# Weight decoding in a Fourier and two-expert kernel: sign taken by a mask and added on GpSimd, two of its buffers closed by time, x queued ahead of weights, start-up and planner prices reordered

## The chip, the cores and the metric

One core of a Trainium2 chip. The metric is the device time of one execution in microseconds (us). The engines are TensorE (PE; its weight loads are PEld), VectorE (DVE), ScalarE (ACT), GpSimd (POOL) and SyncE (SP), which here only issues DMAs. Each works through its own list of instructions in order.

## The reference

```
X = fft(x, axis=1); X = fft(X, axis=2); x = X.real       # x is 2 x 3008 x 256
x = ((1/(1+exp(-(x @ w_gate)))) * (x @ w_val)) @ w_out    # width 1536
h = x @ w_in;  out = (h * cos(h)) @ w_out2                # width 2048, 6016 tokens
```

x is fp32. The host passes the weights as float64, so that the kernel itself turns each into fp32.

## The kernel before

**Stages.** The transform is three rounds of matmuls. Stage A reads x in 16 chunks of 8 matmuls (a pair of chunks is one x load into one of three buffers, `raw`); each fp32 matmul of this stage leaves two records in the trace, 256 in all, and four more come from `xs`. A chunk fills two of PSUM's eight banks, so chunks 3, 7, 11 and 15 use banks 6 and 7. Stage B (12 groups of 8 short matmuls, L405 and L406) and stage C (6 groups of 12, L443) follow, in the order that the string on L473 gives; C writes the transformed tokens into six buffers `eo`. The first expert then runs in 72 steps (`step1`): six token tiles by 12 slices of the hidden width. A step multiplies the two halves (`ab`, L499 to L501, two times six matmuls), DVE combines them (`even`, L517, two instructions; `tokens`, L525, two), ACT takes the sigmoid (L673), GpSimd multiplies (`times`, L529), ACT splits the product (L613, L614), and a GpSimd DMA with addition makes its low part (`lo1`, L552). Four steps later the PE multiplies it by the output weights (`out1`, L539 to L542). The second expert (192 slices, from about 490 us on) is not touched.

**Decoding.** A weight unit is 128 x 512 numbers, 512 KB as float64. SP loads it; ACT takes the magnitude of the high words (L129) and scales the low words (L130); DVE clamps (L113), shifts (L117) and puts the sign in (L135); GpSimd adds the rounding from the low words as integers (L138). A w1 unit then needs a sum and a difference (L159, L160). ACT copies the high part (L143) and DVE or GpSimd subtracts it for the low part (L144). L113 and L117 have one operand in SBUF and one constant in PSUM, which lies at the end of bank 7 (`cmax`, `cmask`); L135 has both operands in SBUF. A chunk that writes bank 7 waits for the last clamp or shift that was recorded ahead of it.

**Order.** Nothing is scheduled at run time. The kernel keeps a clock for each engine (`clk`), and at each stage's slot `fill` puts decode instructions into an engine's list as long as their planned end lies within the slot plus an allowance (`AHA`, `AHB`, `AHC`). A unit is decoded in a buffer that is free for a while: the `eo` buffers until stage C writes them (`ENDS`), and, once stage B has read half of `D1`, four pieces of it (`stages`). Two of those (`ALWAYS`) stay free; the other two are marked `TWO`, since step 2 writes its tokens over them, and whatever is still being decoded there is finished, instruction by instruction, ahead of `tokens` of step 2 on every engine that it needs.

Of the kernel before, what the change touches and what calls it, by code (L numbers as in the profile page):

```python
# [49 lines left out]
def fft_moe_moe(ctx: ExitStack, tc: tile.TileContext, x, x0, head, w1, w1s, wo1, w2, t1, t3, out):  # L50
# [69 lines left out]
    def dec_steps(buf, n):  # L120

        r = buf[:, 0:2 * n].rearrange("p (n t) -> p n t", t=2)
        lo, hi = r[:, :, 0], r[:, :, 1]
        t = buf[:, 2 * n:3 * n]
        u = t.bitcast(U32)

        return [

            (A, .52, lambda: A.activation(out=t, in_=hi, func=AF.Abs, scale=2.0 ** -80)),  # L129
            (A, .52, lambda: A.activation(out=lo.bitcast(I32), in_=lo.bitcast(U32), func=AF.Copy,  # L130
                                          scale=2.0 ** -29)),

            (V, .6, lambda: clamp(t)),
            (V, .6, lambda: shift(u)),
            (V, .6, lambda: V.scalar_tensor_tensor(out=u, in0=hi.bitcast(U32), scalar=0x80000000, in1=u,  # L135
                                                   op0=ALU.bitwise_and, op1=ALU.bitwise_or)),

            (G, 1.23, lambda: G.tensor_tensor(out=t.bitcast(I32), in0=t.bitcast(I32), in1=lo.bitcast(I32),  # L138
                                              op=ALU.add)),
        ]  # L140

    def hilo_steps(hi, lo, src):
        return [(A, .52, lambda: A.copy(hi, src)),  # L143
                (VG, .6, lambda e: e.tensor_tensor(out=lo, in0=src, in1=f32(hi), op=ALU.subtract))]  # L144

# [59 lines left out]
    def fill(e, until):  # L205

        while True:
# [8 lines left out]
            else:  # L216
                if e is DQ and len(todo) > held[0] and clk[e] + 1.5 <= until:
                    for bf in free:
                        if bf[2] <= until and max(clk[e], bf[2]) + LIFE <= bf[1]:
                            start(bf)  # L220
                            break
                    else:
                        return
                    continue
# [24 lines left out]
    LIFE, ALWAYS = 16.0, 1e9  # L249
    TWO = 1e8  # L250
    VADV = 0.5
    ENDS = (44, 52, 54, 62, 70, 70)

    AHA, AHB, AHC = (2, 1.5, 2, 2), (4, 1.5, 3, 1), (3, 1.5, 3, 0)

# [32 lines left out]
    with tc.tile_pool(name="xp", bufs=1) as xp:  # L288
# [23 lines left out]
        DQ.dma_start(out=raws[0][0:96, JC:2 * JC], in_=x[:, 1])  # L312
        G.memset(warm, 0.0)
        V.memset(hd[96:128], 0.0)
        V.memset(cmax, FMAX)
        V.memset(cmask, 0x7FFFFFFF)
        V.memset(hd2, 0.0)
        V.memset(raws[0][96:128], 0.0)
        G.memset(raws[1], 0.0)
        V.memset(raws[2], 0.0)  # L320
        V.memset(xs[96:128], 0.0)
# [4 lines left out]
        for p in range(1, NX2):  # L326
            fill(DQ, clk[DQ] + 2.0)
            load_x2(p)


        for _ in range(NWARM):
            PE.matmul(ps[:, 7, 0:128], warm, warm, start=True, stop=True)

        now = 3.5
        clk[V] = clk[G] = clk[A] = 4.5
        for c in range(NJC):
            if c == 8:
                DQ.dma_start(out=T1, in_=t1)
                DQ.dma_start(out=T3, in_=t3)
                spend(DQ, 1.4)  # L340
            slot(now, 1.71, AHA if c < NJC - 2 else (4, .4, 2, .5) if c < NJC - 1 else (4, .1, 2, -.8))
            b0 = 2 * (c % 4)
# [10 lines left out]
            if c % 2 and c // 2 + NX2 < NJC // 2:  # L353
                clk[DQ] = max(clk[DQ], now + 1.71)
                load_x2(c // 2 + NX2)

            def evac(c=c, b0=b0, at=now + (1.71 if c else 3.4)):
                src = ps[:, b0:b0 + 2, 0:384].rearrange("p a (q c) -> p c a q", c=96)
# [24 lines left out]
            after.append(evac)  # L383
            now += 1.71 if c else 3.4
    now += 1.2
# [13 lines left out]
    def stage_b(b, grp):  # L399
        slot(now, 1.71, AHB)  # L400
        bk = bank()
# [5 lines left out]

        def evac(at=now + 1.71):
            v = ps[:, bk, :].rearrange("p (q s k) -> p s q k", q=4, s=2)
# [21 lines left out]
        after.append(evac)  # L431
        return now + 1.71

    def stage_c(b, ch, ahead=AHB):
        slot(now, 2.54, ahead)
        t = b * NCH + ch
# [3 lines left out]
        def mm(terms, dst):  # L440
# [3 lines left out]

            def evac(at=now + 2.54):
                for un in list(live):
                    if un[1] and un[1][0] is flat[t]:
                        finish(un)
                if clk[V] + .59 < clk[A] + .2:
                    regular(V, .59, at)  # L450
                    V.tensor_copy(dst, o)
                else:
                    regular(A, .47, at)
                    A.copy(dst, o)
# [9 lines left out]
           eo[t][:, 1, 0:PC])  # L464
        return now + 2.54

# [6 lines left out]
    for st in "b00 b01 b02 b03 b04 c00 b05 b10 c01 b11 c02 b12 b13 b14 c10 b15".split():  # L473
# [354 lines left out]
```

## Time and profile before

| | |
|---|---|
| Median of 3 runs | 1028.24 us (1026.69 to 1030.5) |
| Profiled execution | 1028.23 us; its span 1026.3 us |
| Mean granted PE clock | 0.989 of full speed |
| Busy | PE 97%, DVE 75%, ACT 75%, POOL 65% |
| DMA | 85.59 MB, 83 GB/s on average |

Times in the profile count from the span's start; 1.9 us lie outside it. A busy PE is not a PE at its peak, but where its matmuls follow one another without a wait at full clock, the stretch can only be shortened by leaving matmuls out. What other work can move the time lies where PE waits or runs at half clock.

### The profile page before, as it was taken

The page shows a single profiled execution, that of the slowest core. Times are in us where ns is not written, and L with a number is a line of the kernel's source. Part 1 is how long each engine was busy: PE and PEld are TensorE (multiplying, and loading weights), DVE is VectorE, ACT ScalarE, POOL GpSimd, SP SyncE. Part 2 cuts the span into 40 slices and gives each one's busy share as a digit, 9 for nine tenths or more (in the row PEclk, how much of TensorE's full clock was granted, in tenths as well). Part 3 has the DMA queues.
Part 4 walks back from the last instruction along what each step waited for, and adds up shares of the span by engine and source line. Part 5 has one row for each costly group of instructions (what it writes and reads, how often), then busy time and mean ns, then how long its engine had stood idle before and what let it go on. Part 6 is the DMA issues. An engine that isn't in the chain of part 4 may idle for free.

```text
span 1026.3 us, 13186 instructions
## 1 busy us (share of the span) xinstructions
PE 996.3 (97%) x4566; PEld 831.8 (81%) x4566; DVE 770.0 (75%) x1031; ACT 765.4 (75%) x1207; POOL 667.7 (65%) x522
## 2 busy tenths in 40 slices
PE   7996899999999999999999999999999999999998
PEld 7984788887888888878788888888888888888886
DVE  5597887888878878786577777777777777777775
ACT  4675556756667676664788888888888888898886
POOL 3686687967878777775465665756557565665653
PEclk9998899999999999999999999999999999999999
DMA  9612456666676667778500000000000000000000
GB/s 293 226 62 82 81 129 134 141 155 150 146 158 139 136 160 155 187 196 219 130 1 21 1 21 21 1 20 1 21 21 1 21 1 21 0 21 21 1 21 22
DMA packets 25364, 85.59 MB, mean 83 GB/s; under 512 B 3248, under 2 KB 6640, under 8 KB 24624
## 3 DMA queue, kind: packets, MB, share of 16 engines
q0 software_dynamic: 10368, 37.02, 19.0%
q1 hardware_dynamic: 14672, 47.59, 13.6%
q8 instruction: 36, 0.59, 0.3%
q14 instruction: 32, 0.26, 0.1%
q10 hardware_dynamic: 256, 0.14, 0.0%
HBM read 33.16 MB, written 14.56 MB: 46 GB/s over the span
## 4 chain that ended last, share of the span: by engine, by line
PE 87%; DVE 4%; DMA 3%; ACT 2%; issue 2%; POOL 1%; ACTq 0%; SPq 0%; DVEq 0%; POOLq 0%
PE ps L581 25%; PE ps L499 14%; PE ps L500 14%; PE ps L501 14%; PE ps L539 5%; PE ps L541 5%; PE ps L542 5%; DVE D L525 3%; PE ps L349 2%; DMA gh<-D 1%; DMA raw<-in_x_dram 1%; PE ps L443 1%; ACT gh L613 1%; DMA xs<-in_x_dram 1%; PE ps L405 0%
## 5 line engine op out<-in xcount | busy, mean ns | idle before, releaser
L607 POOL TENSOR_TENSOR h<-D,h 128x502 fp32r<-128x502 f32 x191 | 284.2, 1488 | 215.9 <-ACT h L606 204.2
L581 PE MATMUL ps<-h,wr 128*128 128x502 f32 x1152 | 291.8, 389 | 0.0
L499 PE MATMUL ps<-es,wr 128*128 128x502 f32 x672 | 263.8, 393 | 17.3 <-DVE D L525 16.7
L500 PE MATMUL ps<-es,wr 128*128 128x502 f32 x672 | 262.8, 391 | 0.0
L501 PE MATMUL ps<-es,wr 128*128 128x502 f32 x672 | 261.9, 390 | 0.0
L581 PEld LDWEIGHTS ps<-h,wr 128*128 128x128 f32 x1152 | 217.4, 189 | 44.7
L529 POOL TENSOR_TENSOR D<-D 128x502 f32<-128x502 f32 x144 | 184.7, 1326 | 88.5 <-ACT D L673 88.3
L592 DVE SCALAR_TENSOR_TENSOR D<-D,ps 128x502 f32<-128x502 int32 x192 | 130.2, 678 | 117.9 <-POOL h L607 110.5
L525 DVE TENSOR_TENSOR D<-D,ps 128x1004 f32<-128x1004 f32 x144 | 172.9, 1201 | 52.7 <-PE ps L501 32.9
L673 ACT ACTIVATE D<-D 128x1004 f32<-128x1004 f32 x72 | 75.2, 1044 | 138.8 <-DVE D L525 138.7
L499 PEld LDWEIGHTS ps<-es,wr 128*128 128x128 f32 x672 | 127.0, 189 | 46.6 <-DVE D L525 18.8
L593 DVE SCALAR_TENSOR_TENSOR D<-D 128x502 f32<-128x502 int32 x192 | 144.8, 754 | 6.6
L501 PEld LDWEIGHTS ps<-es,wr 128*128 128x128 f32 x672 | 126.9, 189 | 26.6
L591 ACT ACTIVATE D<-ps 128x502 int32<-128x502 f32 x192 | 113.2, 589 | 47.2 <-PE ps L501 45.3
L500 PEld LDWEIGHTS ps<-es,wr 128*128 128x128 f32 x672 | 127.2, 189 | 25.6
L599 DVE TENSOR_TENSOR D<-D,ps 128x502 f32<-128x502 f32 x192 | 128.9, 671 | 16.1 <-ACT D L598 16.1
L597 ACT ACTIVATE D<-D 128x502 f32<-128x502 f32 x192 | 119.2, 621 | 12.2 <-DVE D L593 9.8
L598 ACT ACTIVATE D<-D 128x502 f32<-128x502 f32 x192 | 120.0, 625 | 6.1
L517 DVE SCALAR_TENSOR_TENSOR D<-eo,w,ps 128x502 f32<-128x502 f32 x144 | 102.0, 736 | 23.4 <-PE ps L501 22.9
L606 ACT CAST h<-D 128x502 fp32r<-128x502 f32 x192 | 114.7, 597 | 0.2 <-DVE D L599 0.2
L541 PE MATMUL ps<-gh,wr 128*128 128x502 f32 x288 | 112.5, 391 | 0.0
L542 PE MATMUL ps<-gh,wr 128*128 128x502 f32 x288 | 111.8, 388 | 0.0
(89 smaller groups left out, 1053.4 us busy)
## 6 DMA issues: line engine op xcount, KB each, us to landing
gh<-D POOLq DMA_DIRECT2D x72, 502.0 KB, 4.8
D<-in_w_dram SPq DMA_DIRECT2D x17, 512.0 KB, 4.3
ws<-D SPq DMA_DIRECT2D x16, 512.0 KB, 3.6
wr<-ws SPq DMA_DIRECT2D x16, 512.0 KB, 4.4
out_dram<-D SPq DMA_DIRECT2D x24, 251.0 KB, 3.5
eo<-in_w_dram SPq DMA_DIRECT2D x11, 512.0 KB, 6.4
raw<-in_x_dram SPq DMA_DIRECT2D x15, 256.0 KB, 4.6
D<-in_wo_dram SPq DMA_DIRECT2D x6, 512.0 KB, 3.9
```

The source lines that it names most:

```text
L499: PE.matmul(o, w_hi, m_hi, start=first, stop=False)
L500: PE.matmul(o, w_lo, m_hi, start=False, stop=False)
L501: PE.matmul(o, w_hi, m_lo, start=False, stop=last)
L525: V.tensor_tensor(out=gv[s][:, :, c:c + PC], in0=sas, in1=ps[:, 6:8, 0:PC], op=op)
L529: G.tensor_tensor(out=gv[p][:, 1, m], in0=gv[p][:, 1, m], in1=gv[p][:, 0, m], op=ALU.mult)
L541: PE.matmul(o, WO1[:, f, 0, m], h[:, 0, sl], start=(f == 0), stop=False)
L542: PE.matmul(o, WO1[:, f, 1, m], h[:, 0, sl], start=False, stop=False)
L581: PE.matmul(o, WO2[:, f, i, d * 128:(d + 1) * 128], h[:, m], start=(f == 0 and i == m == 0), stop=(f == NF2 - 1 and m == 1))
L592: V.scalar_tensor_tensor(out=r, in0=k, scalar=-C1, in1=h, op0=ALU.mult, op1=ALU.add)
L593: V.scalar_tensor_tensor(out=r, in0=k, scalar=-C2, in1=r, op0=ALU.mult, op1=ALU.add)
L599: V.tensor_tensor(out=r, in0=r, in1=ps[:, 4 + s % 4, 0:PC], op=ALU.mult)
L607: (V if s == N2S - 1 else G).tensor_tensor(out=h[:, 1], in0=r, in1=f32(h[:, 0]), op=ALU.subtract)
```

## The change

- `dec_steps`: in units whose steps are laid out before the first expert starts (`begun` false), GpSimd adds before DVE sets the sign. In later units DVE masks the sign bit in the high words in place, with a zero from PSUM (`czero`) as its second operand, and GpSimd adds twice: the low words, then the masked high words.
- `hilo_steps`: later units make their low part on GpSimd only, at a planned price of 1.4 us. Copies out of PSUM in stage C go to ACT only once `begun` is set.
- A unit is started in a `TWO` buffer only if it can be planned to end 20.9 us after the end of group b05 at the latest (`two_end`).
- x loads of the first pairs are queued ahead of weights. The zeros of the second and third x buffer are both written by GpSimd. The warming matmuls write bank 6, so that they don't wait for the constants in bank 7.
- Planned prices: 1.79 us for a chunk or a B group (1.71), 2.72 for a C group (2.54); `ENDS`, `AHB` and `beside` differ.

```diff
+        ] + ([
+            (V, .6, lambda: V.scalar_tensor_tensor(out=hi.bitcast(U32), in0=hi.bitcast(U32), scalar=0x80000000,
+                                                   in1=czero.to_broadcast(list(hi.shape)),
+                                                   op0=ALU.bitwise_and, op1=ALU.bitwise_or)),
+            (G, 1.23, lambda: added(lo)),
+            (G, 1.23, lambda: added(hi)),
+        ] if begun[0] else [
+            (G, 1.23, lambda: added(lo)),
             (V, .6, lambda: V.scalar_tensor_tensor(out=u, in0=hi.bitcast(U32), scalar=0x80000000, in1=u,
                                                    op0=ALU.bitwise_and, op1=ALU.bitwise_or)),
-
-            (G, 1.23, lambda: G.tensor_tensor(out=t.bitcast(I32), in0=t.bitcast(I32), in1=lo.bitcast(I32),
-                                              op=ALU.add)),
-        ]
+        ])
...
-        return [(A, .52, lambda: A.copy(hi, src)),
-                (VG, .6, lambda e: e.tensor_tensor(out=lo, in0=src, in1=f32(hi), op=ALU.subtract))]
+        return [(A, .52, lambda: A.copy(hi, src)), (G, 1.4, low) if begun[0] else (VG, .6, low)]
...
-                        if bf[2] <= until and max(clk[e], bf[2]) + LIFE <= bf[1]:
+                        if bf[2] <= until and max(clk[e], bf[2]) + LIFE <= min(bf[1], two_end[0] if bf[1] == TWO else ALWAYS):
...
-    ENDS = (44, 52, 54, 62, 70, 70)
-
-    AHA, AHB, AHC = (2, 1.5, 2, 2), (4, 1.5, 3, 1), (3, 1.5, 3, 0)
+    ENDS = (45.5, 52.5, 57, 65, 73, 73)
+
+    AHA, AHB, AHC = (2, 1.5, 2, 2), (4, 2.5, 4, 2.5), (3, 1.5, 3, 0)
...
-        G.memset(raws[1], 0.0)
-        V.memset(raws[2], 0.0)
+        for r in raws[1:]:
+            G.memset(r, 0.0)
...
-            fill(DQ, clk[DQ] + 2.0)
             load_x2(p)
+            fill(DQ, clk[DQ] + 1.6)
...
-            PE.matmul(ps[:, 7, 0:128], warm, warm, start=True, stop=True)
+            PE.matmul(ps[:, 6, 0:128], warm, warm, start=True, stop=True)
...
-                if clk[V] + .59 < clk[A] + .2:
+                if not begun[0] and clk[V] + .59 < clk[A] + .2:
...
+            two_end[0] = now + 6 * 1.79 + 3 * 2.72 + 2.0
...
-    beside[0] = .5
+    beside[0] = .1
     free[:] = [bf for bf in free if bf[1] == ALWAYS]
+    begun[0] = True
```

On DVE, from the second step of the first expert on (L517 is `even`, L525 `tokens`, L451 a copy of stage C, the rest decoding into wo1), the order was:

```order
L517 SCALAR_TENSOR_TENSOR D_73<-eo_65,w_71,ps 128x502 x2
L525 TENSOR_TENSOR D_73<-D_73,ps 128x2x502 x2
L451 COPY eo_70<-ps 128x502 x2
L517 SCALAR_TENSOR_TENSOR D_73<-eo_65,w_71,ps 128x502 x2
L113 SCALAR_TENSOR_TENSOR D_73<-D_73,ps 128x512
L117 SCALAR_TENSOR_TENSOR D_73<-D_73,ps 128x512
L135 SCALAR_TENSOR_TENSOR D_73<-D_73 128x512
L144 TENSOR_TENSOR wr<-D_73,wr 128x2x256
L113 SCALAR_TENSOR_TENSOR D_73<-D_73,ps 128x512
L117 SCALAR_TENSOR_TENSOR D_73<-D_73,ps 128x512
L135 SCALAR_TENSOR_TENSOR D_73<-D_73 128x512
L144 TENSOR_TENSOR wr<-D_73,wr 128x2x256
L525 TENSOR_TENSOR D_73<-D_73,ps 128x2x502 x2
```

The same place in the changed kernel (`even` is L531, `tokens` L539), from the second step on, up to the first decode instruction:

```order
L531 SCALAR_TENSOR_TENSOR D_73<-eo_65,w_71,ps 128x502 x2
L539 TENSOR_TENSOR D_73<-D_73,ps 128x2x502 x2
L531 SCALAR_TENSOR_TENSOR D_73<-eo_65,w_71,ps 128x502 x2
L539 TENSOR_TENSOR D_73<-D_73,ps 128x2x502 x2
L531 SCALAR_TENSOR_TENSOR D_73<-eo_65,w_71,ps 128x502 x2
L539 TENSOR_TENSOR D_73<-D_73,ps 128x2x502 x2
L531 SCALAR_TENSOR_TENSOR D_73<-eo_65,w_71,ps 128x502 x2
L539 TENSOR_TENSOR D_73<-D_73,ps 128x2x502 x2
L148 SCALAR_TENSOR_TENSOR D_73<-D_73 128x512
```

The eight decode instructions between `even` and `tokens` of step 2 are gone from there; the first one stands behind `tokens` of step 4. The two copies of stage C between the steps are on ACT.

On SP, the first DMAs of the program were (L298 and L306 load x, L152 weights; raw_103, 104 and 105 are the three x buffers, eo_65 to eo_69 the buffers in which weights are decoded):

```order
L310 DMA hd<-in_head_dram 96x480
L311 DMA raw_103<-in_x_dram 96x640
L312 DMA raw_103<-in_x_dram 96x1024
L152 DMA eo_65<-in_w1s_dram 128x48
L152 DMA eo_66<-in_w_dram 128x1024
L298 DMA raw_104<-in_x_dram 32x2048 x3
L152 DMA eo_67<-in_w_dram 128x1024
L298 DMA raw_105<-in_x_dram 32x2048 x3
L152 DMA eo_68<-in_w_dram 128x1024
L306 DMA raw_103<-in_x_dram 96x2048
L152 DMA eo_69<-in_w_dram 128x1024
```

In the changed kernel the same place on SP reads (L311 and L319 load x, L164 weights):

```order
L323 DMA hd<-in_head_dram 96x480
L324 DMA raw_103<-in_x_dram 96x640
L325 DMA raw_103<-in_x_dram 96x1024
L311 DMA raw_104<-in_x_dram 32x2048 x3
L164 DMA eo_65<-in_w1s_dram 128x48
L164 DMA eo_66<-in_w_dram 128x1024
L311 DMA raw_105<-in_x_dram 32x2048 x3
L164 DMA eo_67<-in_w_dram 128x1024
L164 DMA eo_68<-in_w_dram 128x1024
L319 DMA raw_103<-in_x_dram 96x2048
L164 DMA eo_69<-in_w_dram 128x1024
```

The second and the third x pair (raw_104, raw_105) each moved ahead of one w1 unit; the fourth (raw_103 again) has the same three w1 units ahead of it as before.

## Rows read from the trace of the kernel before

**Rows 1.** The page: the span.
```profile
span 1026.3 us, 13186 instructions
```

**Rows 2.** Waits of PE, whole span: who for whom, us, times, longest.
```profile
PE ps L499 <- DVE D L525: 16.7, 5, 11.7
```

**Rows 3.** Timeline of PE, steps 2 to 4: start, duration, instruction, idle before.
```profile
90.53 0.50 PE L499 MATMUL ps<-es,wr 128*128 128x502 f32 x1 [1.16 <-DVE D L525]
...
105.64 0.79 PE L499 MATMUL ps<-es,wr 128*128 128x502 f32 x1 [11.67 <-DVE D L525]
...
112.52 0.39 PE L541 MATMUL ps<-gh,wr 128*128 128x502 f32 x1
```

**Rows 4.** Timeline of DVE in the same stretch.
```profile
88.04 2.44 DVE L525 TENSOR_TENSOR D<-D,ps 128x1004 f32<-128x1004 f32 x2 [2.08 <-PE ps L501]
...
91.57 1.38 DVE L517 SCALAR_TENSOR_TENSOR D<-eo,w,ps 128x502 f32<-128x502 f32 x2
...
92.86 0.69 DVE L113 SCALAR_TENSOR_TENSOR D<-D,ps 128x512 f32<-128x512 f32 x1
...
97.50 0.69 DVE L144 TENSOR_TENSOR wr<-D,wr 128x512 fp32r<-128x512 f32 x1 [2.50 <-ACT wr L143]
...
103.15 2.44 DVE L525 TENSOR_TENSOR D<-D,ps 128x1004 f32<-128x1004 f32 x2
```

**Rows 5.** Timeline of ACT in stage C: three copies out of PSUM.
```profile
74.97 1.55 ACT L454 COPY eo<-ps 128x502 f32<-128x502 f32 x3
```

**Rows 6.** Two late steps: DVE, then GpSimd at the first, then PE after each.
```profile
246.34 5.42 DVE L135 SCALAR_TENSOR_TENSOR D<-D 128x512 uint32<-128x512 uint32 x1
...
445.72 4.88 DVE L135 SCALAR_TENSOR_TENSOR D<-D 128x512 uint32<-128x512 uint32 x1
...
248.02 2.83 POOL L529 TENSOR_TENSOR D<-D 128x502 f32<-128x502 f32 x2
...
252.46 0.49 PE L499 MATMUL ps<-es,wr 128*128 128x502 f32 x1 [0.40 <-DVE D L517]
...
255.77 0.49 PE L499 MATMUL ps<-es,wr 128*128 128x502 f32 x1 [1.69 <-DVE D L525]
...
454.61 0.49 PE L499 MATMUL ps<-es,wr 128*128 128x502 f32 x1 [1.67 <-DVE D L525]
```

**Rows 7.** Groups by line and shape: busy, mean ns of one, idle before.
```profile
L135 DVE SCALAR_TENSOR_TENSOR eo<-eo 128x512 uint32<-128x512 uint32 x11 | 10.5, 957 | 0.3
...
L117 DVE SCALAR_TENSOR_TENSOR D<-D,ps 128x512 uint32<-128x512 uint32 x23 | 15.6, 680 | 0.1
```

**Rows 8.** Timeline of PE in stage A.
```profile
10.98 2.89 PE L349 MATMUL ps<-hd,raw 128*128 128x96 f32 x24 [1.65 <-DMA raw<-in_x_dram]
...
14.20 2.92 PE L349 MATMUL ps<-hd,raw 128*128 128x96 f32 x24 [0.34 <-DVE eo L117]
...
21.22 21.25 PE L349 MATMUL ps<-hd,raw 128*128 128x96 f32 x160 [1.87 <-DMA raw<-in_x_dram]
```

**Rows 9.** Stretches: us, PE, PEld, DVE, ACT, POOL busy (instructions), granted clock, DMA.
```profile
21.20:27.60 6.40, 6.38 (x30) 6.40 (x31) 4.36 (x10) 3.25 (x5) 3.25 (x4) 0.50 0.64 236
...
28.00:42.00 14.00, 14.00 (x128) 14.00 (x127) 5.91 (x8) 9.09 (x14) 8.75 (x8) 1.00 0.92 322
...
60.00:70.00 10.00, 10.00 (x69) 9.15 (x68) 9.93 (x21) 6.07 (x16) 9.12 (x9) 1.00 0.01 2
...
140.00:200.00 60.00, 60.00 (x265) 49.65 (x264) 48.38 (x54) 40.00 (x49) 47.53 (x42) 1.00 0.62 136
```

**Rows 10.** Timeline of SP and of ACT: second and third w1 unit, issued and landed.
```profile
7.29 0.58 SPq L152 DMA_DIRECT2D eo<-in_w_dram  x1
...
10.26 0.58 SPq L152 DMA_DIRECT2D eo<-in_w_dram  x1
...
12.02 0.68 ACT L129 ACTIVATE eo<-eo 128x512 f32<-128x512 f32 x1 [1.18 <-DMA eo<-in_w_dram]
...
17.76 0.68 ACT L129 ACTIVATE eo<-eo 128x512 f32<-128x512 f32 x1 [3.00 <-DMA eo<-in_w_dram]
```

More of the change, by code (lines that the diff above doesn't have):

```diff
@@ L104, in fft_moe_moe @@
     VG = (V, G)
+    begun = [False]
     def spend(e, us, after=0.0):
@@ L110, in fft_moe_moe @@
     cmax, cmask = ps[:, 7, 510:511], ps[:, 7, 511:512].bitcast(U32)
+    czero = ps[:, 7, 509:510].bitcast(U32)
     def clamp(t):
@@ L125, in dec_steps, with added @@
         u = t.bitcast(U32)
+        def added(w):
+            G.tensor_tensor(out=t.bitcast(I32), in0=t.bitcast(I32), in1=w.bitcast(I32), op=ALU.add)
         return [
@@ L134, in dec_steps, with low @@
             (V, .6, lambda: shift(u)),
+        ] + ([
[6 more added lines that the diff above has]
+            (G, 1.23, lambda: added(lo)),
             (V, .6, lambda: V.scalar_tensor_tensor(out=u, in0=hi.bitcast(U32), scalar=0x80000000, in1=u,
                                                    op0=ALU.bitwise_and, op1=ALU.bitwise_or)),
-            (G, 1.23, lambda: G.tensor_tensor(out=t.bitcast(I32), in0=t.bitcast(I32), in1=lo.bitcast(I32),
-                                              op=ALU.add)),
-        ]
+        ])
     def hilo_steps(hi, lo, src):
-        return [(A, .52, lambda: A.copy(hi, src)),
-                (VG, .6, lambda e: e.tensor_tensor(out=lo, in0=src, in1=f32(hi), op=ALU.subtract))]
+        def low(e=G):
+            e.tensor_tensor(out=lo, in0=src, in1=f32(hi), op=ALU.subtract)
+        return [(A, .52, lambda: A.copy(hi, src)), (G, 1.4, low) if begun[0] else (VG, .6, low)]
     ws = [dpool.tile([128, 2 * UC], F32, name=f"ws{u}") for u in range(NF2)]
@@ L250, in fft_moe_moe @@
     TWO = 1e8
+    two_end = [TWO]
     VADV = 0.5
-    ENDS = (44, 52, 54, 62, 70, 70)
-    AHA, AHB, AHC = (2, 1.5, 2, 2), (4, 1.5, 3, 1), (3, 1.5, 3, 0)
+    ENDS = (45.5, 52.5, 57, 65, 73, 73)
+    AHA, AHB, AHC = (2, 1.5, 2, 2), (4, 2.5, 4, 2.5), (3, 1.5, 3, 0)
     ess = [cpool.tile([128, 2, 2, PC], F32R, name="es0")]
@@ L313, in fft_moe_moe @@
         G.memset(warm, 0.0)
+        for c_, k_ in ((cmax, FMAX), (cmask, 0x7FFFFFFF), (czero, 0)):
+            V.memset(c_, k_)
+        V.memset(hd2, 0.0)
         V.memset(hd[96:128], 0.0)
-        V.memset(cmax, FMAX)
-        V.memset(cmask, 0x7FFFFFFF)
-        V.memset(hd2, 0.0)
         V.memset(raws[0][96:128], 0.0)
-        G.memset(raws[1], 0.0)
-        V.memset(raws[2], 0.0)
+        for r in raws[1:]:
+            G.memset(r, 0.0)
         V.memset(xs[96:128], 0.0)
@@ L340, in fft_moe_moe @@
                 spend(DQ, 1.4)
-            slot(now, 1.71, AHA if c < NJC - 2 else (4, .4, 2, .5) if c < NJC - 1 else (4, .1, 2, -.8))
+            slot(now, 1.79, AHA if c < NJC - 2 else (4, .4, 2, .5) if c < NJC - 1 else (4, .1, 2, -.8))
             b0 = 2 * (c % 4)
@@ L353, in fft_moe_moe, with evac @@
             if c % 2 and c // 2 + NX2 < NJC // 2:
-                clk[DQ] = max(clk[DQ], now + 1.71)
+                clk[DQ] = max(clk[DQ], now + 1.79)
                 load_x2(c // 2 + NX2)
-            def evac(c=c, b0=b0, at=now + (1.71 if c else 3.4)):
+            def evac(c=c, b0=b0, at=now + (1.79 if c else 3.4)):
                 src = ps[:, b0:b0 + 2, 0:384].rearrange("p a (q c) -> p c a q", c=96)
@@ L383, in fft_moe_moe @@
             after.append(evac)
-            now += 1.71 if c else 3.4
+            now += 1.79 if c else 3.4
     now += 1.2
@@ L399, in stage_b @@
     def stage_b(b, grp):
-        slot(now, 1.71, AHB)
+        slot(now, 1.79, AHB)
         bk = bank()
@@ L406, in stage_b, with evac @@
             PE.matmul(o, D1[:, b * 48 + 24 + k2, :], T1[:, 1], start=False, stop=True)
-        def evac(at=now + 1.71):
+        def evac(at=now + 1.79):
             v = ps[:, bk, :].rearrange("p (q s k) -> p s q k", q=4, s=2)
@@ L431, in stage_b @@
         after.append(evac)
-        return now + 1.71
+        return now + 1.79
     def stage_c(b, ch, ahead=AHB):
-        slot(now, 2.54, ahead)
+        slot(now, 2.72, ahead)
         t = b * NCH + ch
@@ L443, in mm, with evac @@
                 PE.matmul(o, w, m, start=(i == 0), stop=(i == len(terms) - 1))
-            def evac(at=now + 2.54):
+            def evac(at=now + 2.72):
                 for un in list(live):
@@ L464, in stage_c @@
            eo[t][:, 1, 0:PC])
-        return now + 2.54
+        return now + 2.72
     def consts():
```

## The prediction

> **What bounds the kernel now.** The span is 1026.3 us [rows 1], 1.9 us less than the 1028.23 us of the same execution, which is also the median of the three runs (1028.24), so sums against it are sums against the median. PE is nearly always busy, so I read its waits first. One entry stands out: `ab` waiting for DVE's `tokens`, 16.7 us in five waits [rows 2]. The timeline places them: 1.16 and 11.67 us in steps 2 and 3 of the first expert [rows 3], 1.69 and 1.67 us far later, each in a single step [rows 6]; 0.5 us is left. DVE's own list explains the large one: `tokens` of step 1 end at 90.48, `even` of step 2 at 92.95, and then, instead of `tokens`, DVE goes through two weight units of decoding, waiting in between for ACT and GpSimd, until `tokens` start at 103.15 [rows 4]. The two late ones each follow one L135 of about 5 us [rows 6], which otherwise takes under 1 us [rows 7].
>
> The third place is stage A: idle times of 1.65, 0.34 and 1.87 us [rows 8], and after the last of them 6.4 us at half clock, in which PE does 30 records where it later does 128 in 14.0 us [rows 9]. That is 0.213 us against 0.109 a record, 3.1 us lost. All of this together, about 26 us, is what the change can reach.
>
> **First expert, steps 1 to 4.** By the order, no decoding stands between `even` and `tokens` any more. I walk the chain from the old times. `tokens` of step 1 end at 90.48. `even` 2 takes 1.38, to 91.9; PE's six matmuls of half a step take 6 x 0.226 = 1.36 (60 us for 265 matmuls, [rows 9]) from 90.53, also to 91.9. `tokens` 2 take 2.44, 92.0 to 94.4; the second half of step 3 runs 94.5 to 95.9, `even` 3 beside it. `tokens` 3: 95.9 to 98.3; second half of step 4: 98.4 to 99.8. Then `out1` of step 0 starts at 99.8 instead of 112.52 [rows 3]: 12.7 us earlier, part of it the half clock that followed the 11.67 us. From there a step has 24 matmuls, 5.4 us, against 3.8 us of DVE, so PE leads again. Against it: all three copies of a C group are now on ACT, behind the sigmoid, and the next C group needs the banks. Three such copies take 1.55 us [rows 5]; the wait is between 0 and that, and I take 1.0, since nothing on ACT hides them. The chain leaves PE three gaps of about 1.1 us (2.44 less 1.36); should they bring half clock once, that is another 3.1 us. Term: -11.7, between -12.7 and -8.6.
>
> **First expert, the two late steps.** The new sign instruction has one operand in SBUF and one in PSUM, as L117 has, which averages 0.68 us over 23 with no long one among them, where L135 averages 0.96 [rows 7]. So 0.40 + 1.69 + 1.67 = 3.76 us of PE waits go [rows 6]. The second GpSimd addition (an integer addition, about 1.3 us by its neighbours of the same size) lies beside other work: GpSimd is busy 47.53 of 60 us here [rows 9], and 20 units times some 2 us spread over 390 us lift it by about a tenth. If that cover were gone, `lo1` would be late by the excess of a step; it is issued about two steps ahead of its use. Term: -3.7, between -3.8 and 0. A gain beyond is excluded, since PE doesn't wait elsewhere in this stage.
>
> The Trainium skill, page "SBUF — State Buffer", section "Who interferes with whom", has it that a DVE instruction with two SBUF inputs blocks against a GpSimd instruction that reads SBUF, and one with a single SBUF input doesn't. This case agrees on which lines suffer (L135, not L117), but the page's block lasts one instruction, while 5.42 us is longer than the two multiplications in it together, 2.83 [rows 6]. If a single instruction were the whole lock, something else would be behind those two waits; that is the third rival.
>
> **Stage A.** Here the order speaks two ways. The second x pair moves ahead of a w1 unit, but it still waits for earlier small loads to land; its last third, and with it the pair, comes perhaps 0.75 us sooner than 10.9, at 10.2. The second half of chunk 3 writes bank 7 and waits for the last clamp or shift recorded ahead of it: before, the shift of the second w1 unit (0.34 us of waiting, [rows 8]); now that unit's clamp, one instruction earlier. But that unit's load now stands behind the third x pair, where the third unit stood: issued about half a microsecond ahead of that one's 10.26, at 9.75, instead of 7.29 [rows 10]. The one landed 4.7 us after its issue (12.0), the other 7.5 (17.76) [rows 10]; so it lands between 14.5 and 17.3. I take 15.2, nearer the first, since the same x pair is in front of it but less behind it. With 0.68 on ACT [rows 10] and 0.69 on DVE [rows 4] the clamp ends at 16.6. PE is there at 10.2 + 24 x 0.109 = 12.8: it idles 3.8 us, longer than the 1.87 that preceded the half clock. Taken as half clock again, 30 records take to 23.0, the other 14 of this x pair and `xs` to 24.5. The fourth pair, bound by loads to about 21 as before (the same weights are ahead of it), no longer waits, and its 32 records end at 28.0; in the old run they ended at 27.85 (30 by 27.6, two more at full clock). Nothing is gained. Chunk 7 then waits in the same way for the fourth unit's clamp, behind DVE instructions that wait for GpSimd: 0 to 1.8 us, I take 1.0. Term: +1.2. If no half clock comes and the load lands early, -3; if it lands late and half clock comes twice, +6. Zeros on GpSimd (1.8 us each) follow one another from the start on and end some 4 us before the x load that they gate; the earlier warming ends ahead of data that come no sooner. Both cost nothing.
>
> **Stages B and C.** PE's work is unchanged and was almost free of waits. DVE is full: 9.93 of 10 us [rows 9]. It has two decode instructions and some copies fewer here, but sums and differences moved from GpSimd to it: by the order 19 instructions with two SBUF operands from the last copy of stage A to the first `even`, where there were 11. At L135's excess of 0.27 us [rows 7] eight more cost 2.2 us of DVE, mostly in gaps where DVE waits. Term: +0.5, between -0.8 (less waiting for low parts) and +4 (all of that on PE's path and a late copy beside it).
>
> **Sum.** 1028.2 - 11.7 - 3.7 + 1.2 + 0.5 = 1014.5; I say 1014.
>
> **Rivals.**
> - *x first works.* PE doesn't meet the clamp, and the idle times and the half clock of stage A go: 1.65 + 0.34 + 1.87 + 3.1 = 7.0 at most; with 5 of it, 1014.5 - 1.2 - 5 = 1008. For it: x is earlier in the queue. Against it: the bank 7 wait is in the program, and its load is later. 0.20.
> - *Decoding late.* DVE's extra waits reach PE in stage C or at the first use of the second wo1 unit (step 6, with little more than 1 us in hand by my walk), with one half clock: +3.5 + 3.1, 1021. For it: DVE at 99% in the rows. Against it: its list has fewer instructions. 0.17.
> - *The late steps stay* (the lock is not their cause, or a sign instruction laid out early meets GpSimd in step 5): +3.7, 1018. 0.08.
> - *Slower.* PE waits for clamps not only at chunk 3 but at 7, 11 and 15, 3.8 us each and 3.1 of half clock after each: 6.9 an event. One is in the forecast; two more bring 1014.5 to 1028, level, and three bring 1035. For it: all four chunks have this wait. Against it: the later units' loads have no x pair moved ahead of them. 0.05.
> - The forecast itself: 0.50. That the change doesn't act is excluded by the order for steps 2 and 3.
>
> **How the numbers follow.** About 0.5% (5.1 us) is what a measurement of this kernel can tell from no change: faster means below 1023, slower above 1033. Below 1023 lie the forecast, x first, the late steps and two thirds of decoding late: 0.89. Slower: 0.05. The rest, 0.06, is within. For the range I take the forecast with its bounds, x first down to 1007, and the better half of decoding late, to 1021.5: 0.8.
>
> **What would show it.** Steps right: no decode line between `even` and `tokens` of steps 1 to 4, no PE wait over 1.5 us there, and the first `out1` some 12 us nearer to the first `ab`. Late steps right: no DVE sign instruction over 1.5 us once the expert runs, and no wait of PE there. Stage A right: PE's longest idle time in front of the second half of chunk 3, released by DVE's clamp, and half clock after it; wrong if stage A ends before 40 or after 46, where it ended at 42.5 (21.22 + 21.25, [rows 8]). Stages B and C wrong if PE waits over 2 us in them. The whole is wrong if the wait for `tokens` comes back under another line.

## The result, and the profile after

The changed kernel takes 1042.76 us (median of 4, 1042.44 to 1047.38), the kernel before 1027.47 beside it (1025.89 to 1030.50): a ratio of 1.0146, 95% interval 1.0115 to 1.0178. It is slower by about 15 us where 14 fewer were predicted. The profiled execution took 1043.01 us, its span is 1041.0 us, 14.7 more than in [rows 1].

In the program after, `even` is L531, `tokens` L539, `ab` L513 to L515, `out1` L553 to L556, `times` L543, the clamp L115, the shift L119, the sign with two SBUF operands L148, the mask L141, the GpSimd additions L130, a unit's high part L156 and low part L154.

The prediction did not use the view that shows most here: the start of `tokens` in each step, after less before. Where the difference stays level, the two kernels run at the same pace, so each change of it is a place where time went or came. (`tokens` is DVE's. At step 0 PE's own lag, by its first `ab`, is 3.7 us; its bank wait of 1.46 us in step 1 then brings it up to DVE's.)

| `tokens` of step | before, us | after less before | what lies between |
|---|---|---|---|
| 0 | 81.05 | +5.1 | start, stages B and C |
| 3 | 108.56 | -6.8 | the stall of [rows 3] is gone: -11.9 |
| 6 | 123.78 | -1.3 | step 5: +5.5 |
| 10 | 145.62 | -1.4 | level |
| 11 | 150.92 | +4.9 | `out1` in step 10: +6.3 |
| 13 | 162.02 | +8.9 | `out1` in step 12: +4.0 |
| 15 | 172.87 | +17.5 | `out1` in step 14: +8.6 |
| 28 | 243.98 | +17.6 | level |
| 66 | 456.44 | +12.9 | the two late steps of [rows 6] are gone: -4.6 |
| end of span | 1026.3 | +14.7 | a DMA behind `lo1` late, once: +1.8 |

PE's waits, longest totals first (who for whom, us, times, longest); [rows 2] had one entry of 16.7:

```profile
PE ps L555 <- ACT wr L156: 6.0, 3, 4.9
PE ps L362 <- DVE eo L115: 4.9, 2, 3.3
PE ps L556 <- POOL wr L154: 4.7, 3, 2.3
PE ps L513 <- DVE D L119: 3.7, 1, 3.7
PE ps L513 <- DVE D L539: 3.5, 3, 1.2
PE ps L553 <- DMA gh<-D: 2.9, 1, 2.9
```

The wait for `tokens` is down to three gaps. The first and third entry are new: `out1` waits for the high and the low part of a wo1 unit. PE's timeline shows where (the first three rows answer to [rows 3]):

```profile
95.96 0.49 PE L513 MATMUL ps<-es,wr 128*128 128x502 f32 x1 [1.16 <-DVE D L539]
...
104.28 0.49 PE L513 MATMUL ps<-es,wr 128*128 128x502 f32 x1 [1.16 <-DVE D L539]
...
105.76 0.39 PE L555 MATMUL ps<-gh,wr 128*128 128x502 f32 x1
...
114.36 0.49 PE L513 MATMUL ps<-es,wr 128*128 128x502 f32 x1 [3.67 <-DVE D L119]
...
144.72 0.49 PE L555 MATMUL ps<-gh,wr 128*128 128x502 f32 x1 [0.57 <-ACT wr L156]
...
147.54 0.79 PE L556 MATMUL ps<-gh,wr 128*128 128x502 f32 x1 [2.33 <-POOL wr L154]
...
161.72 0.50 PE L555 MATMUL ps<-gh,wr 128*128 128x502 f32 x1 [0.56 <-ACT wr L156]
...
164.04 0.79 PE L556 MATMUL ps<-gh,wr 128*128 128x502 f32 x1 [1.82 <-POOL wr L154]
...
181.26 0.79 PE L555 MATMUL ps<-gh,wr 128*128 128x502 f32 x1 [4.87 <-ACT wr L156]
...
182.61 0.79 PE L556 MATMUL ps<-gh,wr 128*128 128x502 f32 x1 [0.56 <-POOL wr L154]
```

The six waits from 144.72 on add up to 10.7 us. The rest of the 18.8 is half clock after them, by the stretches (columns as in [rows 9], which had 60.00 of 60 at 1.00 from 140 to 200):

```profile
140.00:170.00 30.00, 24.72 (x88) 19.23 (x87) 16.10 (x19) 13.76 (x16) 20.48 (x18) 0.83 0.47 104
170.00:200.00 30.00, 24.57 (x97) 19.54 (x96) 18.44 (x23) 15.03 (x19) 15.76 (x15) 0.89 0.34 74
```

A mean clock of 0.83 over 30 us is half clock for 34% of it, 10.2 us in which 5.1 are lost; 0.89 gives 3.3 more. Together that is 19.1, about the 18.8 that the steps show; it is an estimate, since some of the half clock lies in the waits themselves. From 200 to 500 us PE is busy in every stretch of 100 (100.00 each; before 97.92 from 200 to 300), and the long sign instructions of [rows 6] are gone; the mask takes 681 ns on the mean (groups as in [rows 7]):

```profile
L141 DVE SCALAR_TENSOR_TENSOR D<-D,ps 128x512 uint32<-128x512 uint32 x20 | 13.6, 681 | 0.0
```

Why the units are late: the high parts of wo1 units 0 to 5 (ACT's timeline) come 14.8 to 19.5 us apart from the second on, while `out1` opens a new unit in every second step, every 10.9 us:

```profile
84.14 0.62 ACT L156 CAST wr<-D 128x512 fp32r<-128x512 f32 x1 [2.48 <-DVE D L148]
...
113.02 0.62 ACT L156 CAST wr<-D 128x512 fp32r<-128x512 f32 x1 [1.48 <-DVE D L148]
...
127.79 0.60 ACT L156 CAST wr<-D 128x512 fp32r<-128x512 f32 x1
...
144.06 0.60 ACT L156 CAST wr<-D 128x512 fp32r<-128x512 f32 x1
...
161.07 0.60 ACT L156 CAST wr<-D 128x512 fp32r<-128x512 f32 x1
...
180.59 0.62 ACT L156 CAST wr<-D 128x512 fp32r<-128x512 f32 x1 [0.60 <-POOL D L130]
```

The kernel before decoded no faster. Its DVE did one decode instruction a step once the expert ran (clamp, shift, sign, next unit's clamp):

```profile
115.08 0.68 DVE L113 SCALAR_TENSOR_TENSOR D<-D,ps 128x512 f32<-128x512 f32 x1
...
120.58 0.68 DVE L117 SCALAR_TENSOR_TENSOR D<-D,ps 128x512 uint32<-128x512 uint32 x1
...
126.13 0.69 DVE L135 SCALAR_TENSOR_TENSOR D<-D 128x512 uint32<-128x512 uint32 x1
...
131.60 0.68 DVE L113 SCALAR_TENSOR_TENSOR D<-D,ps 128x512 f32<-128x512 f32 x1
```

That is a unit in three steps, 16.4 us. It had the lead that it needed, since four buffers and the 11.67 us stall itself had finished four of the six units by 103 us. SP had issued the last three wo1 loads between 82.13 and 84.98 us; in the changed kernel it issues them between 113.13 and 143.29. The change took away the stall and the lead together.

### The profile page after: what moved, and what is told of

The parts are those of the page before. It is cut to its first block, busy times and chain, and to the rows that moved or that the text cites. A ratio compares the mean times of both kernels' runs of the same rounds, so it can differ in the third digit from the quotient of the medians.

```text
span 1041.0 us, 13179 instructions
## 1 busy us (share of the span) xinstructions
PE 1004.5 (96%) x4566; PEld 837.1 (80%) x4566; DVE 761.8 (73%) x1033; ACT 769.6 (74%) x1213; POOL 688.1 (66%) x535
## 4 chain that ended last, share of the span: by engine, by line
PE 83%; DVE 5%; POOL 4%; issue 3%; DMA 3%; ACT 2%; SPq 0%; DVEq 0%; POOLq 0%; ACTq 0%
PE ps L595 25%; PE ps L513 14%; PE ps L514 14%; PE ps L515 13%; PE ps L556 6%; PE ps L553 6%; PE ps L555 5%; DVE D L539 2%; DMA gh<-D 1%; POOL D L130 1%; POOL wr L154 1%; POOL D L543 1%; ACT gh L627 1%; PE ps L456 1%; ACT gh L628 1%
## 5 line engine op out<-in xcount | busy, mean ns | idle before, releaser
L513 PE MATMUL ps<-es,wr 128*128 128x502 f32 x672 | 263.0, 391 | 7.2 <-DVE D L119 3.7
L515 PE MATMUL ps<-es,wr 128*128 128x502 f32 x672 | 261.4, 389 | 0.0
L543 POOL TENSOR_TENSOR D<-D 128x502 f32<-128x502 f32 x144 | 186.9, 1361 | 58.7 <-ACT D L687 56.9
L539 DVE TENSOR_TENSOR D<-D,ps 128x1004 f32<-128x1004 f32 x144 | 172.9, 1201 | 50.0 <-PE ps L515 30.7
L513 PEld LDWEIGHTS ps<-es,wr 128*128 128x128 f32 x672 | 127.0, 189 | 34.7 <-DVE D L539 4.7
L515 PEld LDWEIGHTS ps<-es,wr 128*128 128x128 f32 x672 | 126.7, 189 | 26.4
L531 DVE SCALAR_TENSOR_TENSOR D<-eo,w,ps 128x502 f32<-128x502 f32 x144 | 101.4, 735 | 48.7 <-PE ps L515 48.1
L555 PE MATMUL ps<-gh,wr 128*128 128x502 f32 x288 | 115.8, 402 | 6.0 <-ACT wr L156 6.0
L556 PE MATMUL ps<-gh,wr 128*128 128x502 f32 x288 | 115.8, 402 | 4.7 <-POOL wr L154 4.7
```

Source lines behind the costliest of these rows:

```text
L513: PE.matmul(o, w_hi, m_hi, start=first, stop=False)
L515: PE.matmul(o, w_hi, m_lo, start=False, stop=last)
L539: V.tensor_tensor(out=gv[s][:, :, c:c + PC], in0=sas, in1=ps[:, 6:8, 0:PC], op=op)
L543: G.tensor_tensor(out=gv[p][:, 1, m], in0=gv[p][:, 1, m], in1=gv[p][:, 0, m], op=ALU.mult)
L555: PE.matmul(o, WO1[:, f, 0, m], h[:, 0, sl], start=(f == 0), stop=False)
L556: PE.matmul(o, WO1[:, f, 1, m], h[:, 0, sl], start=False, stop=False)
```

## The experiments

The theories tried against one another on the late units: **ROOMS** (two buffers instead of four make wo1 units late), **CHAIN** (three passes through GpSimd make them late), **LOCK** and **ORDER** (the one long sign instruction, or the place of the steps), and **PACE** (the planner's allowances). Times are medians. Ratios are to the kernel before on the same chip, which took 1028.95 us beside e1 to e4, 1027.08 beside e5, e6, e7 and f1, and 1029.8 beside e9 and f2 to f4. The changed kernel was timed beside 1027.47 only, so a difference to it is safer by the ratios than by the medians.

**Buffers open again (e1).** In the changed kernel:

```
-  ... + LIFE <= min(bf[1], two_end[0] if bf[1] == TWO else ALWAYS):
+  ... + LIFE <= bf[1]:
```

> The changed kernel with the time limit on the two TWO buffers taken out again; all else stays. Two theories for the waits of out1 for wo1 units in steps 10, 12 and 14 (the tokens of steps 11, 13 and 15 start 6.2, 4.1 and 8.6 us later against before than those of the steps ahead of them, 18.8 together). Theory ROOMS: the units come late because two buffers instead of four are left to decode in. Then here they come in time by the order (highs of units 1 to 5 behind the sigmoids of steps 2, 2, 5, 8 and 10 or one earlier, first used in steps 6, 8, 10, 12 and 14): 18.8 us go, the knock-on of 1.9 at the end too, but five decode instructions with two round trips over GpSimd stand ahead of tokens of step 2 again: +8 to +11. Time 1028 to 1036. Theory CHAIN: the units come late because a unit begun in the first expert now goes three times through GpSimd (two additions and the low part); then the waits stay and the stall of step 2 is added: 1050 or more.

1036.09 us, ratio 1.0069 (1.0041 to 1.0098). `out1` waits for no unit any more: the difference of `tokens` to before is level from step 6 (+10.5) to step 28 (+10.2). In its place the old stall is back, PE's timeline:

```profile
110.99 0.79 PE L513 MATMUL ps<-es,wr 128*128 128x502 f32 x1 [11.31 <-DVE D L539]
...
125.88 0.79 PE L513 MATMUL ps<-es,wr 128*128 128x502 f32 x1 [3.02 <-DVE D L115]
```

ROOMS holds. The time is just past its upper end of 1036, since step 5 still loses about 5 us (second row).

**The closing alone, in the kernel before (e3).** The same limit, with its own prices:

```
-  ... + LIFE <= bf[1]:
+  ... + LIFE <= min(bf[1], two_end[0] if bf[1] == TWO else ALWAYS):
...
+  two_end[0] = now + 6 * 1.71 + 3 * 2.54 + 2.0
```

> The kernel before with the time limit alone added (with its own planned prices). Both theories expect the 11.67 us stall ahead of tokens of step 2 to go (tokens of step 3 some 12 us earlier). ROOMS: units 2 to 5 come late (highs behind the sigmoids of steps 7, 10, 12 and 14, first used in steps 8, 10, 12 and 14), some 15 to 20 us lost in steps 8 to 15: 1027.5 - 12 + 18 = 1033, between 1029 and 1038. CHAIN: a unit with one GpSimd addition is fast enough: 1016 to 1020.

1054.87 us, ratio 1.0233 (1.0189 to 1.0277): worse than either theory. ROOMS has the kind right but gave 1038 at most; CHAIN, which gave 1016 to 1020, falls as the whole cause. The stall goes (`tokens` of step 3: -10.1), and then steps 8 to 14 lose 31 us (to +21.2 in step 15), with one GpSimd addition per unit. PE waits for each unit's high part:

```profile
142.65 0.50 PE L543 MATMUL ps<-gh,wr 128*128 128x502 f32 x1 [4.26 <-ACT wr L143]
...
164.32 0.79 PE L543 MATMUL ps<-gh,wr 128*128 128x502 f32 x1 [6.58 <-ACT wr L143]
...
185.30 0.79 PE L543 MATMUL ps<-gh,wr 128*128 128x502 f32 x1 [6.57 <-ACT wr L143]
```

A further 8.6 us went between steps 30 and 66, at two long sign instructions of the kind in [rows 6] (DVE's timeline); after the first, PE ran at half clock for 6.8 us.

```profile
333.16 6.97 DVE L135 SCALAR_TENSOR_TENSOR D<-D 128x512 uint32<-128x512 uint32 x1
...
404.69 5.43 DVE L135 SCALAR_TENSOR_TENSOR D<-D 128x512 uint32<-128x512 uint32 x1
```

**The mask alone, in the kernel before (e4).** `dec_steps` and `hilo_steps` use the new steps once `begun` is set, at the place of the change; `czero` comes with them, nothing else.

```
+        ] + ([ <mask on DVE, two additions on GpSimd> ] if begun[0] else [ <as before> ])
...
+    begun[0] = True
     step1(0)
```

> The kernel before with the new decode steps alone, in units laid out once the first expert runs (mask in place, two GpSimd additions, low part on GpSimd); four buffers as before. ROOMS: wo1 units stay in time (all but the last two are decoded by step 3), the stall of step 2 stays (11 to 14 us), the two late locks of 3.8 us go: 1022 to 1027. CHAIN: the last two units become late too: over 1030.

1024.49 us, ratio 0.9954 (0.994 to 0.9968). The stall stays, units are in time, and the two late steps give 2.9 and 2.0 us by the difference of `tokens`. This part of the change does what it should, by itself.

**The old decode steps, buffers closed (e2).**

```
-        ] if begun[0] else [
+        ] if False else [
...
-  (G, 1.4, low) if begun[0] else (VG, .6, low)]
+  (VG, .6, low)]
```

> The changed kernel with the old decode steps throughout: the sign by the two-operand DVE instruction (in the order in which the change leaves it for units laid out early, GpSimd addition first), one GpSimd addition, the low part on DVE or GpSimd. The closing of the two buffers and all else stay. ROOMS: units 3 to 5 are as late (the order has them behind the sigmoids of steps 10, 12 and 14), the locks of the late steps can come back: 1042.8 and 0 to +6, so 1042 to 1049. CHAIN: most of the 18.8 us go and the locks of the late steps cost 3.7 again: 1027 to 1032.

1046.71 us, ratio 1.0164 (1.0126 to 1.0203). That is in the range of ROOMS, but partly by luck: ROOMS had the units as late as in the changed kernel, and the profile of e2 lost 9.1 us to them instead of 18.8. It lost 5.8 more in its start, and some 4.5 from step 19 to step 66, where the changed kernel gains 4.6 (long sign instructions are back there, up to 4.87 us). So a shorter chain does help, by about half of what the late units cost; but the kernel before with the same closing, and one addition per unit as well, lost 31, so the chain's length does not decide.

**Lock or order (e6, e9).** First the new steps for all wo1 units, which changes the order too:

```
+  steps += dec_steps(buf, n, begun[0] or kind == "wo1")
```

> The changed kernel with the new decode steps for all wo1 units, those laid out ahead of the first expert too, so that no sign instruction with two SBUF operands is left in it (in the changed kernel one of them takes 4.52 us in step 5, and tokens of steps 5 and 6 lose 5.5 us there). Theory LOCK: the 5.5 us go and stay gone, 1037; by the order unit 1 is done by step 1 and units 2 to 5 each come up to a step sooner, which can bring it to 1030. Theory GIVEN BACK: units 2 to 5 come when they come, and what step 5 saves is waited for in steps 10 to 14: 1041 to 1044.

1024.59 us, ratio 0.9982 (0.9968 to 0.9997): 18 us better than the changed kernel by the medians, 17 by the ratios, far more than either theory gave. Step 5 loses almost nothing, unit 1 is done at 93 us instead of 115, and of the late units one pair of waits is left, 0.56 and 2.31 us in step 14. The high parts of units 1 to 5 come no faster (17.4 us apart on the mean, 16.9 in the changed kernel), but the first of them 23 us earlier: it is the lead that is back, not the rate. Then the sign of the early wo1 units alone exchanged in its place, the order left as it was:

```
-  (V, .6, <sign, two SBUF operands>),
+  (V, .6, (lambda: (masked(), added(hi))) if kind == "wo1" else <sign, two SBUF operands>),
```

> The changed kernel, its order and plan untouched; only in wo1 units laid out ahead of the first expert the sign instruction with two SBUF operands is replaced, in the same place of DVE's list, by the mask, with the GpSimd addition of the masked words directly behind it (not planned for). e6 changed form and order of these units at once and won 18 us; this tells which. Theory ORDER: the lock costs only what tokens of steps 5 and 6 lose (5.5 us), units 3 to 5 stay late because their order is as before: 1037 to 1039. Theory CASCADE: the 4.5 us of the one locked instruction delay its buffer and with it all later units: the lateness in steps 10 to 14 goes with it, 1022 to 1027.

1035.61 us, ratio 1.0059 (1.0038 to 1.0079). By the medians 7 of the 18 us are the lock and 11 the order, by the ratios 9 and 8. In the profile step 5 loses 0.1 us, and the waits for the units are as they were (L560 and L561 are `out1`, L161 and L159 high and low part here), from -6.1 in step 8 to +10.6 in step 15: 16.7 us of the 18.8.

```profile
PE ps L560 <- ACT wr L161: 6.0, 3, 4.9
...
PE ps L561 <- POOL wr L159: 4.6, 4, 1.9
```

So CASCADE falls and ORDER holds, though its range began at 1037. The old form of unit 1 goes from DVE to GpSimd and back to DVE, each in a later step's slot, and keeps its buffer until step 5; the next unit of that buffer starts that much later: SP issues the load of unit 3 at 113.13 us in the changed kernel, at 115.39 in e9 and at 89.12 in e6.

**Pace (e7).** In the changed kernel, both buffers closed and all decode steps kept:

```
+    SOON = {V: 3, G: 6, A: 4}
...
-        fill(e, until + LATE[e])
+        fill(e, until + (SOON if s < 14 else LATE)[e])
```

> The changed kernel with other planning allowances for decoding in steps 0 to 13 of the first expert (DVE 3 us instead of 1.2, GpSimd 6 instead of 4.5, ACT 4 instead of 2); the two buffers stay closed, and every decode step is as it was. By the order no decode instruction stands ahead of tokens of step 2, and units 1 to 5 are done one to four steps ahead of their first use. Theory PACE (ROOMS made finer: two buffers are enough if decoding may run further ahead; what was lost is that the planner with two buffers still allowed it only about a unit in three steps, where out1 uses one in two): the 18.8 us and the knock-on of 1.9 at the end go, 0 to 4 us come as tokens that wait for decode instructions: 1020 to 1027. Theory TRAFFIC (the extra GpSimd work and the DVE instructions beside it are the bound, whatever the order): the waits move from out1 to even and tokens, 1036 or more.

1020.53 us, ratio 0.9939 (0.9918 to 0.9961): PACE holds, and TRAFFIC falls, though GpSimd (the fifth pair) is busy 54.8 us of these 60 where it was 47.53 in [rows 9]:

```profile
140.00:170.00 30.00, 30.00 (x133) 24.64 (x132) 24.79 (x30) 20.73 (x25) 29.33 (x26) 1.00 0.64 143
170.00:200.00 30.00, 30.00 (x133) 24.83 (x132) 23.66 (x27) 20.23 (x25) 25.47 (x24) 1.00 0.68 154
```

PE waits for no unit and never leaves full clock there. Two buffers and the longer chain are enough, if decoding may run further ahead. Its high parts of units 1 to 5 come at 93.58, 114.79, 123.14, 142.08 and 148.84 us. That is 13.8 apart on the mean, still slower than one in 10.9, but from a start 19 us earlier, which is lead enough for the few units that there are.

**Stage A (e5).** Chunks over banks 0 to 5, so that none meets a clamp:

```
-            b0 = 2 * (c % 4)
+            b0 = 2 * (c % 3)
```

> The changed kernel with stage A's chunks over banks 0 to 5 (three pairs) instead of all eight, so that no chunk writes bank 7 and none waits for a clamp or shift. Theory CLAMP: the two waits ahead of chunks 3 and 7 (3.27 and 1.61 us in the profile of the changed kernel, 5.42 and 1.61 in that with the old sign) with the half clock after the first are lost time: stage B starts at 39 to 41 instead of 43.5, the time is 1038 to 1040.5, and its scatter (1042.4 to 1047.4) shrinks. Theory LOADS: the x transfers bind this stage anyhow (its last pair lands when it did): stage B starts at 42.5 to 43.5 and the time stays at 1042 to 1043.

1042.6 us, ratio 1.0153 (1.0125 to 1.018). CLAMP falls: stage B starts at 43.98, and at 43.37 to 44.48 in the three profiles below with the same banks and x first. LOADS has the time right, but not the reason: x loads hold PE for 1.18 us only. PE waits for no clamp, but as long for ACT (PE's timeline; L365 multiplies `xs`):

```profile
20.00 0.72 PE L365 MATMUL ps<-hd,xs 128*128 128x96 f32 x4 [3.93 <-ACT D L375]
...
36.00 7.36 PE L362 MATMUL ps<-hd,raw 128*128 128x96 f32 x64 [1.18 <-DMA raw<-in_x_dram]
```

ACT's timeline shows the cause. Its copies of chunks (L375) stand behind the first decode instruction of a unit (L134), which waits for that unit's load; in the changed kernel the clamp stood behind the same:

```profile
16.27 0.66 ACT L134 ACTIVATE eo<-eo 128x512 f32<-128x512 f32 x1 [3.72 <-DMA eo<-in_w_dram]
16.84 0.79 ACT L375 COPY D<-ps 128x768 f32<-128x768 f32 x1
```

The bank was the place of the wait, the late weight load its cause.

**Together (f1).** Six banks, the mask for all wo1 units and the wider allowances:

> The three edits together: stage A over six banks, the new decode steps for all wo1 units, the wider allowances in steps 0 to 13. If they add up as CLAMP, LOCK and PACE say: 1022 for the pace, less 3 for the lock (part of it went with the pace), less 3 for stage A: 1016, between 1011 and 1021, faster than the kernel before. If LOADS and GIVEN BACK hold: 1021 to 1025.

1017.42 us (1016.78 to 1018.17), ratio 0.9908 (0.9887 to 0.9929): faster than both kernels, though little under the pace alone. The 3 us between the two lie ahead of step 0 (`tokens` +4.1 against +7.7 in e7), where the start-up scatters; from step 0 to step 28 it gains 10.1 us and e7 10.9. So neither the mask nor the six banks is shown to add to the pace. Its waits, beside those of the changed kernel above:

```profile
PE ps L513 <- DVE D L539: 4.0, 3, 1.4
PE ps L365 <- ACT D L375: 3.7, 1, 3.7
PE ps L456 <- ACT D2h L438: 1.9, 1, 1.9
```

Three kernels built on it looked at the 4 us by which step 0 is still late (allowances of stages B and C, f2 and f3) and at the start (f4).

```
-    AHA, AHB, AHC = (2, 1.5, 2, 2), (4, 2.5, 4, 2.5), (3, 1.5, 3, 0)
+    AHA, AHB, AHC = (2, 1.5, 2, 2), (4, 2, 4, 1.8), (3, 1.5, 3, 0)
```

> The three edits of the run before (allowances, mask for wo1 units, six banks), and in stages B and C smaller planning allowances for ACT and DVE (2 and 1.8 us instead of 2.5 each). In that run tokens of step 0 began 4.1 us later than in the kernel before, though stage B began at the same time; PE's waits for D2h and D2l copies, behind decoding on ACT and DVE, are 3.2 us of it. By the order two wo1 units are done ahead of the first expert, the others by steps 1, 2, 5 and 7, and nothing stands ahead of tokens of step 2. If the allowances made the copies late: 1013 to 1016. If DVE is simply full in these stages and the lag is its work: 1017 to 1020.

1019.08 us (1014.73 to 1022.18), ratio 0.9902 (0.9866 to 0.9937). Step 0 stays late (+4.6): the wait for D2h falls from 1.9 to 0.6, but that for D2l rises from 1.3 to 2.4, and one of 1.4 for the copies of the last C group comes. Stage B started at 44.48 here and at 43.37 in f1; counted from there the lag is 3.5 us against 4.1, so the smaller allowances mostly move it.

```
-    AHA, AHB, AHC = (2, 1.5, 2, 2), (4, 2.5, 4, 2.5), (3, 1.5, 3, 0)
+    AHA, AHB, AHC = (2, 1.5, 2, 2), (4, 2.5, 3, 2.5), (3, 1.5, 3, 0)
```

> The three edits, and in stages B and C GpSimd's planning allowance back at 3 us (4 in the changed kernel), ACT's and DVE's left at 2.5. By the order sums and differences go to DVE or GpSimd differently and units 1 to 5 are done by steps 1, 1, 3, 6 and 8. If GpSimd's allowance made the lag of 4.1 us ahead of step 0: 1013 to 1015. If ACT's and DVE's did: 1017 to 1019.

1017.07 us (1013.24 to 1018.14), ratio 0.9878 (0.9849 to 0.9908). In its profile step 0 is late by 2.4 instead of 4.1 (by 2.0 counted from stage B's start, 43.84), in the time little is seen: not settled.

```
-            load_x2(p)
-            fill(DQ, clk[DQ] + 1.6)
+            fill(DQ, clk[DQ] + 2.0)
+            load_x2(p)
...
-  PE.matmul(ps[:, 6, 0:128], warm, warm, start=True, stop=True)
+  PE.matmul(ps[:, 7, 0:128], warm, warm, start=True, stop=True)
```

> The three edits with the start-up of the kernel before (weights queued ahead of the second and third x pair, the zeros and the constants in the old order and on the old engines, warming matmuls in bank 7). If queueing x first brings nothing, stage B starts between 42 and 44 (43.4 with x first) and the time is 1016 to 1020, the rest being small changes of order further on. If it brings what the rival 'x first works' had (5 us), stage B starts at 47 or later and the time is 1021 or more. A stage B that starts ahead of 42 would say that x first costs time.

1022.67 us, ratio 0.9938 (0.9919 to 0.9958). Stage B starts at 46.38 instead of 43.37, between the two cases: by this profile x first is worth 3 us in this form of the kernel, which the scatter told below leaves uncertain. A wait of 4.3 us for the copies of the last C group came too, so that not all of the loss (5.3 us by the medians, 3.1 by the ratios) is the start.

## Why the prediction was wrong, step by step

- **Steps 1 to 4, -11.7:** right. From step 0 to step 3 the difference falls by 11.9, with three gaps of 1.16 and no half clock; the bank wait for ACT's copies took 1.46 instead of 1.0. By PE it is a little less: the first `out1` is 10.5 us nearer to the first `ab`, where some 12 were named as the sign. PE is late by 3.7 at its first `ab` and comes to DVE's +5.1 only by that bank wait.
- **Two late steps, -3.7:** right, and larger by the difference of `tokens` (-4.6, and as much with the mask alone).
- **Stage A, +1.2:** right in its mechanism. The longest wait stands ahead of chunk 3, released by the clamp, with half clock after it; chunk 7 waits as said; and nothing is gained, as stage B starts at 43.49 against 43.38, so the rival *x first works* falls. The half clock was put at 6.4 us and lasts 3.4 (16.9 to 20.3 us). One profile is weak evidence for the size: with this start-up five others have stage B at 43.90 to 49.54 (last section), with the old one two others have 43.68 and 41.93 (e3, e4). The load that the clamp waits for was put at 15.2 us and ACT takes it up at 14.93; PE's wait was put at 3.8 and is 3.27:

```profile
16.36 4.55 PE L362 MATMUL ps<-hd,raw 128*128 128x96 f32 x24 [3.27 <-DVE eo L115]
...
27.44 15.46 PE L362 MATMUL ps<-hd,raw 128*128 128x96 f32 x136 [1.61 <-DVE eo L115]
...
43.49 0.49 PE L418 MATMUL ps<-T,D 128*128 128x128 f32 x2 [0.60 <-ACT D L380]
```

- **Stages B and C, +0.5:** mis-sized, inside its bounds but wrong by its own sign (PE waits over 2 us): the first `ab` starts at 80.57 instead of 76.88, +3.6 beside stage A, and PE waits 3.8 us in these stages (1.4 before). The prediction counted DVE's two-operand instructions; the longest wait there was 1.56 us for an ACT copy. What makes the lag is not settled (f2, f3).
- **Step 5:** the clause in the third rival ("a sign instruction laid out early meets GpSimd in step 5") came true, but with no price of its own. It cost 5.5 us there and 7 to 9 in all (e9), which the sum did not have.
- **The step that failed:** "From there a step has 24 matmuls, 5.4 us, against 3.8 us of DVE, so PE leads again." It asks whether DVE has room in a step, not whether the weights of `out1` are there. The rival *decoding late* came nearest, but put the lateness down to DVE's extra waits, looked at one unit, the second, and priced one wait with one half clock, 6.6 us. Units 3, 4 and 5 were late, one after the other, for 18.8 us, because a stream slower than its user falls behind at each use once its lead is gone. The rival *slower* had the direction, but by clamps: chunk 7 waited 1.61 us and chunks 11 and 15 not at all. Both rates stood in the trace of before: DVE's decode rows one step apart, and a new unit every second step.
- **The end, not foreseen:** w2 units are decoded later too (the first one is stored at 211.99 instead of 170.28 us), their last loads are issued closer together, and one DMA of `lo1` is late by 2.92 us instead of 1.00. The late units alone don't explain that wait: it is 2.5 in e1, where none was late, and 1.0 in e2. Its cause stays open.

The sum with the measured terms: +5.1 - 11.9 + 5.5 + 18.8 - 4.6 + 1.8 = +14.7, the difference of the spans.

## What to carry to other kernels

When a change removes a stall, ask what was being produced during the stall and who uses it later; compare the producer's rate and its lead with the user's rate over the whole stretch, not only at the first use. In a kernel ordered by a planner, the start of one recurring instruction, after less before, step by step, shows where the time went. A buffer that is closed and an allowance that paces decoding have to be set together: with wider allowances (e7) the changed kernel gains 6.5 us where it had lost 15.

## What the runs showed of the hardware

A DVE instruction with two SBUF operands can be held for longer than one GpSimd instruction. In step 5 it took 4.52 us, where its kind takes 0.68 alone; first DVE, then GpSimd in the same stretch of the changed kernel:

```profile
108.47 4.52 DVE L148 SCALAR_TENSOR_TENSOR D<-D 128x512 uint32<-128x512 uint32 x1
```

```profile
108.47 1.55 POOL L154 TENSOR_TENSOR es<-eo,es 128x502 fp32r<-128x502 f32 x1
109.77 2.66 POOL L543 TENSOR_TENSOR D<-D 128x502 f32<-128x502 f32 x2
```

Three GpSimd instructions follow one another from 108.47 to 112.43 us, and the DVE instruction ends 0.56 us after the last. The mask with its constant in PSUM, put in the same place (e9), took 0.68 us, and the loss of step 5 went from 5.5 us to 0.1. The Trainium skill, page "SBUF — State Buffer", section "Who interferes with whom", has the kinds of instructions right and says, there of DVE's two-port modes, that whoever issues first keeps the other blocked for the whole instruction; here the block lasted over three of them. Nor did an earlier start help: the two long ones of e3 began 0.43 and 0.44 us ahead of GpSimd's first computing instruction (333.59 and 405.13) and still took 6.97 and 5.43 us, though GpSimd was issuing a DMA just then.

The start-up scatters: with one and the same list of loads and of instructions in stage A, six profiles (the changed kernel, e1, e2, e6, e7 and e9) show waits of 3.27, 3.40, 5.42, 3.53, 4.21 and 3.71 us ahead of chunk 3, and stage B starting at 43.49, 43.90, 49.54, 44.68, 45.92 and 44.66. A gain of 2 us in stage A can't be read from one profile.
